# Two transformer layers in one launch: flat reads for the sums of squares, a hinted branch on SyncE, and four pieces of work in other places

## The chip, the cores and the metric

The kernel runs on one core of a Trainium2 chip. Its engines are TensorE (PE in the profile; its weight loads are listed apart, as PEld), VectorE (DVE), ScalarE (ACT), GpSimd (POOL) and SyncE (SP), which here only issues DMAs. Each engine runs its own instructions in their order and waits for the others by semaphores. The metric is the device time of one launch in microseconds, the median of the runs.

## The reference

Two layers, each an attention block and a gated block, with the same weights in both layers. There are 2048 tokens, 448 features, 16 heads of 28 features, 1792 hidden features, all in float32.

```python
x = A_x                                             # 1 x 2048 x 448
for layer in range(2):
    qkv = layernorm(x) @ wqkv                       # 448 x 1344, 16 heads
    p = softmax(q @ k.T * 28 ** -0.5)               # 2048 x 2048 for each head
    x = x + (p @ v) @ wo
    y = layernorm(x)
    x = x + (sigmoid(y @ w_gate) * (y @ w_up)) @ w_down
```

## The kernel before

**Number formats.** Most products are made of float16 halves: an operand is a high part and the rest that the high part leaves, and three products of such parts add up to one. A weight matrix is scaled by a power of two that comes from the sum of its squares; the exact sum does not matter, only its binary exponent.

**Stages of a layer.** `project` makes the heads' queries, keys and values, for four blocks of 512 tokens. `attend` runs over the 16 heads and in each over 16 chunks of 128 keys. `out_project` applies `wo`. `gated` runs over the four blocks and, in each, over seven pairs of hidden tiles. The order of the instructions on every engine is the order in which the program writes them; nothing is rescheduled, except that `attend` works out from a rule how far the second products may run.

**Products by seven.** In `gated`, and for most of the queries and keys of layer 1, a product of 2 x 2 quarters is made with seven products and sums of quarters. A block's operands for that are made by its *half steps*, in `half_steps`: `r11`, `t1`, `t2`, `t3` and so on, each a subtraction or two on DVE (lines 443, 459 and 462) and a conversion on ACT (lines 451 and 453). The first of them, `r11`, is the first that reads the block's transposed values `xraw`, and so it waits for the DMA that gathers them. The half steps of a next block are laid between the products of a current one: `portions` says how many of them stand at each of six points (0 to 5) of each pair. Within a pair of `gated`, point 2 lies just ahead of the additions on DVE (line 1956) that read the banks `side`, and point 5 at the pair's end, behind the sums of hidden operands (lines 1831 to 1838).

**From layer 0 to layer 1.** The end of `gated` also prepares the next layer. `go_on` is called between the last second products and issues on SP: the store of the third block's transposed values (`xt_scr`, line 389), their gather (`xraw`, lines 397 and 399), and the load of the value weights (`wv`, line 740). SP's DMAs are issued in order; one that waits holds back those behind it. In `project` of layer 1, `vals(0, ...)` makes the values of the first block (line 1071) and `vals(1, ...)` those of the second (lines 641 to 643), into PSUM banks 3, 0, 1 and 6. Bank 6 held the squared norms `qnorm` of the second block's queries; `fin` takes their maxima on DVE (line 859).

**The branch.** A flag that DVE computes decides whether exact row maxima are needed. It is read by every engine (line 1211), which then branches (line 1212, not into the long body in these runs). Behind the branch SP issues the load of a head's guard rows (line 773), which the first scores of the first head need. `expect_jump` puts a branch hint into the program for PE: for layer 0's branch at the program's start, for layer 1's behind layer 0's branch.

**Attention.** Score units (128 keys by 512 queries, line 1507, banks `sc`) are taken three at a time; ACT makes their exponentials (line 1522), PE multiplies these with the values (line 1558). A few units of each head go *aside*: DVE makes their exponentials with a polynomial (lines 1532 to 1541). `ASIDE` says at which chunk of a head an aside unit is scored, and which chunk and query block it is; the bank `aside` is the one in which the head before kept its result, so it is free once DVE has read that (line 1587). The same DVE queue also prepares the weights of `gated` and of layer 1 during layer 0's attention: first sums of squares (class `Measure`, line 1268, before attention, and class `Prepare`, line 1398, in heads 0 and 1), then splits into sums of quarters (lines 255 to 264).

**Reads for the sums of squares.** A part of a matrix is read as rows on partitions, with `load_rows`: three DMAs for 448 rows, the last 64 rows twice (lines 216 and 219).

Of the kernel before, what the change touches and what calls it, by code (L numbers as in the profile page):

```python
# [12 lines left out]
BF16 = mybir.dt.bfloat16  # L13
F16 = mybir.dt.float16
I32 = mybir.dt.int32
AF = mybir.ActivationFunctionType
# [3 lines left out]
P = 128  # L20
S = 2048
D = 448
# [7 lines left out]
NF = F // P  # L30
# [36 lines left out]
ASIDE = {1: ((6, 15, 1),), 2: ((4, 10, 3), (9, 15, 1)), 3: ((4, 9, 3), (8, 13, 1), (12, 15, 2))}  # L67
FEW = "2222222222222223"


TAIL = (0, 1, 3, 2, 5, 4, 6)

PAIRS_QK = ((0, 1), (4, 5), (2, 6))
ALONE = 3
SUMS_AT = ((("w", 3), 74), (("u", 0), 122), (("u", 6), 236))

# [46 lines left out]
def interleaved_layers(ctx: ExitStack, tc: tile.TileContext, x_in, wqkv, wo, w_gate, w_up,  # L123
                       w_down, out):
    nc = tc.nc
# [87 lines left out]
    def load_rows(dst, src, c0, n, queue=nc.sync, second=None):  # L213

        for a, b in ((0, 2), (2, 3)) if second else ((0, 3),):
            (second if a else queue).dma_start(
                dst[:, a:b, :], src[a * P:b * P, c0:c0 + n].rearrange("(s p) n -> p s n", p=P))
        for r in (0, 64):
            (second or queue).dma_start(dst[r:r + 64, 3, :], src[384:448, c0:c0 + n])

    def split(hi, lo, raw):
# [559 lines left out]

    def expect_jump(layer):

        tc.mark_branch_hint_location(f"loose{layer}", hint="LikelyTaken",
                                     engines=[mybir.EngineType.PE])

# [6 lines left out]
    def project(layer, wq, begun):  # L793
# [355 lines left out]
        else:  # L1149
# [85 lines left out]
    class Measure:  # L1235
# [9 lines left out]
        def read(self, n=1):  # L1245
            for _ in range(n):
                kind, j = self.to_read.popleft()
                t = big.get("raw", [P, 2048])
                n = {"o": 4, "d": min(4, NF - 4 * j), "gu": 0}[kind]
                v = t[:, 0:n * D].rearrange("p (s n) -> p s n", n=D)  # L1250
                queue = nc.sync if kind == "o" or j < 3 and kind == "d" else nc.gpsimd
                if kind == "gu":
# [8 lines left out]
                self.rows.append((kind, t, n * D))  # L1261

        def add(self):
            kind, t, n = self.rows.popleft()
            m, n = {"o": (3, n), "d": (6, n), "gu": (4, 1024)}[kind]
            v = t[:, 0:n]
            junk = big.get("junk", [P, 2048], BF16)
            nc.vector.tensor_tensor_reduce(junk[:, 0:n], v, v, 1.0, sums[:, m:m + 1],
                                           op0=ALU.mult, op1=ALU.add,
                                           accum_out=self.part[:, 0:1])  # L1270
            big.put_next(junk)
            nc.vector.tensor_copy(sums[:, m:m + 1], self.part[:, 0:1])
            if kind == "gu":
                junk = qrt.get("junk", [P, 1024], BF16)
                nc.scalar.activation(junk, t[:, 1024:2048], AF.Square, accum_out=sums[:, 5:6])
                qrt.put(junk)
            big.put(t)
# [26 lines left out]
    class Prepare:  # L1304
# [41 lines left out]
        def read(self, kind, j):  # L1346
# [25 lines left out]
        def view(self, t, kind):  # L1372
            if kind == "gu":
                return t.rearrange("p (w s c) -> p w s c", w=2, s=4)
            if kind in "guq":
# [103 lines left out]
    def attend(layer, values, heads, last_values, gate, wq):  # L1479
# [294 lines left out]
    def gated(layer, first, wt, wq):  # L1774
# [311 lines left out]
        if not last:  # L2086
# [48 lines left out]
    def portions(b, p):  # L2135
# [100 lines left out]
```

## Time and profile before

| what | value |
|---|---|
| median of 3 runs | 1892.09 us (1891.86 to 1894.91) |
| the profiled execution's own time | 1893.09 us |
| its span, first to last instruction | 1891.4 us |
| granted TensorE clock | 1.000 |
| PE busy, PEld busy | 1879.7 us (99%), 1378.1 us (73%) |
| DVE busy, ACT busy, POOL busy | 1482.7 us (78%), 1418.5 us (75%), 250.9 us (13%) |
| DMA | 278.70 MB, mean 147 GB/s |

Times inside the run are microseconds from the span's start. Layer 0's projection runs to about 118, its attention to about 568, its gated part to about 956; layer 1's projection runs to about 1054. In a row of the timeline stand the start, the duration, the engine, the line and operation, the tiles, how many equal instructions are merged, and in brackets the idle time before with what ended it. Matmuls overlap their successors, so a row's start is surer than its end.

### The profile page before, as it was taken

Reading aid. Unit: us, or ns where it says so; the run is one execution under the profiler, and the core shown is the slowest. Engines: PE = TensorE matmul, PEld = TensorE weight load, DVE = VectorE, ACT = ScalarE, POOL = GpSimd, SP = SyncE. Lnnn points to the kernel's source line nnn. Section 1 sums busy time; section 2 is a strip of 40 time slices with the busy share of each in tenths; the row PEclk is TensorE's granted clock in tenths of the full one; section 3 lists DMA queues with packets and bytes.
Section 4 is the critical chain, followed back from the end, with each engine's and each line's share of the span. In section 5 each row is a group of like instructions: output and inputs, shape, how many; then the busy total and the mean of one; then the engine's idle time right before and its main releaser. Section 6 shows DMA issues by size and latency. Waiting matters only on the chain. (4 is left out here: it accounts for less than half of the span.)

```text
span 1891.4 us, 57180 instructions
## 1 busy us (share of the span) xinstructions
PE 1879.7 (99%) x24531; PEld 1378.1 (73%) x24531; DVE 1482.7 (78%) x2996; ACT 1418.5 (75%) x1873; POOL 250.9 (13%) x487
## 2 busy tenths in 40 slices
PE   9999999999999999999999999999999999999999
PEld 4456655556556899998977566765568768999999
DVE  7758999998997887787767587787778688877664
ACT  6569999999993655555557899999999747555541
POOL 3023122222202111111110000000000021111110
PEclk9999999999999999999999999999999999999999
DMA  7676454344333755646573421122110256566553
GB/s 251 190 217 160 133 159 124 121 134 127 115 108 87 267 199 213 221 185 245 192 222 117 102 52 45 34 52 52 29 49 17 74 164 227 200 228 223 209 208 142
DMA packets 117335, 278.70 MB, mean 147 GB/s; under 512 B 14574, under 2 KB 72686, under 8 KB 116944
## 3 DMA queue, kind: packets, MB, share of 16 engines
q0 software_dynamic: 33616, 165.92, 24.5%
q1 hardware_dynamic: 82304, 107.66, 20.1%
q8 instruction: 194, 3.18, 0.7%
q10 hardware_dynamic: 1152, 1.38, 0.3%
q14 instruction: 69, 0.57, 0.1%
HBM read 213.43 MB, written 53.08 MB: 141 GB/s over the span
## 5 line engine op out<-in xcount | busy, mean ns | idle before, releaser
L1522 ACT ACTIVATE prob_s<-sc 128x1536 f32<-128x1536 f32 (+1 forms) x657 | 888.8, 1479 | 8.7 <-PE sc L1507 6.7
L1558 PE MATMUL acc<-prob_s,val_s 128*32 128x256 f32 (+3 forms) x7700 | 579.5, 384 | 0.8 <-issue 0.8
L1507 PE MATMUL sc<-qp_s 114*32 114x512 f16 x7868 | 562.4, 379 | 0.2 <-DMA qp_s<-qk_scr 0.2
L631 PEld LDWEIGHTS <-gu_s 128*128 128x128 f16 x4368 | 426.8, 98 | 48.4 <-issue 2.5
L1507 PEld LDWEIGHTS <-qp_s 114*32 114x32 f16 x8192 | 290.2, 95 | 191.0 <-issue 80.8
L1558 PEld LDWEIGHTS acc<-prob_s,val_s 128*32 128x32 f32 x7700 | 291.9, 110 | 126.9 <-issue 12.1
L631 PE MATMUL chain<-xwide_s,gu_s 128*128 128x256 f16 x2016 | 247.5, 273 | 0.0
L1867 PE MATMUL dnp<-dn_s,hparts_s 128*128 128x224 f16 x2184 | 245.9, 259 | 0.0
L1867 PEld LDWEIGHTS <-hparts_s 128*128 128x128 f16 x2184 | 210.2, 98 | 5.1
L1538 DVE SCALAR_TENSOR_TENSOR power_q<-power_q,expo_q 128x512 f32<-128x512 f32 x243 | 168.2, 692 | 8.3
L1940 ACT COPY one_q<-chain 128x256 f32<-128x256 f32 x224 | 82.1, 372 | 112.4 <-PE chain L631 111.9
L1956 DVE TENSOR_TENSOR one_q<-side,one_q 128x512 f32<-128x512 f32 x112 | 72.1, 685 | 94.7 <-PE side L631 94.5
L631 PE MATMUL side<-xshort_s,gu_s 128*128 128x256 f16 x1120 | 140.6, 273 | 2.4 <-DVE one_q L1956 2.4
L1748 POOL DMA_DIRECT2D gu_s<-gu_parts x104 | 55.9, 538 | 441.6 <-PE side L631 427.6
L1820 ACT CAST hparts_s<-hsums_q 128x256 f16<-128x256 f32 (+1 forms) x152 | 71.5, 485 | 37.2 <-DVE hsums_q L1832 23.6
L1558 PE MATMUL acc<-power_q,val_s 128*32 128x256 f32 (+3 forms) x300 | 94.2, 396 | 0.0
L631 PE MATMUL side<-xwide_s,gu_s 128*128 128x256 f16 x672 | 91.7, 273 | 0.0
L1587 DVE STREAM_TRANSPOSE oturned_q<-acc 128x512 f32<-128x512 f32 x32 | 22.9, 717 | 82.4 <-PE acc L1558 82.1
L616 PE MATMUL qkp<-xhl_s,wqk_s 128*128 128x512 f16 x385 | 86.6, 379 | 0.9 <-ACT wqk_s L236 0.6
L1967 ACT ACTIVATE one_q<-one_q 128x512 f32<-128x512 f32 x56 | 35.3, 630 | 63.8 <-DVE one_q L1956 63.6
L1532 DVE TENSOR_SCALAR expo_q<-aside,base 128x512 f32<-128x512 f32 x81 | 60.5, 747 | 22.2 <-PE aside L1507 21.7
L1824 DVE TENSOR_TENSOR hparts_s<-hsums_q,hparts_s 128x256 f16<-128x256 f32 (+1 forms) x152 | 72.6, 516 | 6.0 <-ACT hparts_s L1820 6.0
(259 smaller groups left out, 2393.9 us busy)
## 6 DMA issues: line engine op xcount, KB each, us to landing
gu_s<-gu_parts POOLq DMA_DIRECT2D x104, 800.0 KB, 6.0
dn_s<-dn_parts POOLq DMA_DIRECT2D x42, 784.0 KB, 7.5
qp_s<-qk_scr SPq DMA_DIRECT2D x96, 224.0 KB
gu_parts<-pack_s POOLq DMA_DIRECT2D x14, 800.0 KB, 3.8
xt_scr<-xs_s SPq DMA_DIRECT2D x48, 224.0 KB
xraw_s<-xt_scr SPq DMA_DIRECT2D x12, 768.0 KB
qk_scr<-qkhl_q SPq DMA_DIRECT2D x35, 256.0 KB
qp_s<-qk_scr SPq DMA_DIRECT2D x64, 112.0 KB
```

Of the source, the lines that this page charges most:

```text
L616: nc.tensor.matmul(pm, w, x, start=(i == 0), stop=(i == len(terms) - 1))
L631: nc.tensor.matmul(pm, a, x, start=(first and i == 0), stop=(i == len(terms) - 1), skip_group_check=True)
L1507: nc.tensor.matmul(ps[32 * j:32 * j + 32, :], hd.k[:, keys], hd.q[:, qb * W:(qb + 1) * W], start=True, stop=True, tile_position=(0, 32 * j))
L1522: nc.scalar.activation(prob[:, 0:n, :], ps[:, 0:n, :], AF.Exp, scale=exp_scale)
L1532: nc.vector.tensor_scalar(y, ps, base2[:, 0:1], -126.0, op0=ALU.mult, op1=ALU.max)
L1538: nc.vector.scalar_tensor_tensor(p, p, c[k], y, op0=ALU.add, op1=ALU.mult)
L1558: nc.tensor.matmul(acc[qb * VC:(qb + 1) * VC, s], v[:, kc % TB, h, :], probs[c * NB + qb][:, s], start=(kc == 0 and a == 0), stop=(kc == N ...
L1820: nc.scalar.copy(to[:, :, 0], a)
L1824: nc.vector.tensor_tensor(to[:, :, 1], a, to[:, :, 0], op=ALU.subtract)
L1867: nc.tensor.matmul(pm, a[:, x, t], w[:, p, y], start=(begin and n == 0 and (j == 0 or alone)), stop=(n == 2), skip_group_check=True)
L1940: nc.scalar.copy(to, pm)
L1956: nc.vector.tensor_tensor(one[m], side[m], one[m], op=ALU.add)
```

## The change

- **Flat reads.** For the sums of squares a weight matrix is read as one flat run of memory cut into 128 equal pieces, one for each partition: one DMA of 128 x 896 numbers (`CHUNK`) where three stood, 128 x 1568 for `wo`, three of 128 x 1792 and one of 128 x 896 for `w_down`. No row is read twice. The reductions on DVE become 896 wide where they were 1024, and 1568 where `wo`'s was 1792.
- **SP's hint.** Behind layer 0's branch SP too gets a hint for layer 1's branch.
- **A half step.** In pair 3 of the last block of layer 0's `gated`, the half step at point 2 goes to point 5. It is `r11` of the next layer's first block.
- **Value weights.** `load_values` is called ahead of `third.gather`, no longer behind it.
- **Norm maxima.** In `vals(1, ...)` of layer 1, `fin` stands ahead of the half step `h3[2]` (`t2` of the last block), no longer behind it.
- **Asides of head 8.** In layer 0's head 8 the two aside units are scored at chunks 5 and 10; they were at 4 and 9. Which units they are does not change.

```diff
+BEHIND_SUMS = 8, ((5, 10, 3), (10, 15, 1))
+CHUNK = D * NF // 7
...
+    def flat(w):
+        return w.rearrange("r c -> (r c)").rearrange("(p n) -> p n", p=P)
...
-    def expect_jump(layer):
+    def expect_jump(layer, also=[]):
...
-                                     engines=[mybir.EngineType.PE])
+                                     engines=[mybir.EngineType.PE] + also)
...
-            vals(1, b1, {0: both(*h3[0:2]), 1: both(h3[2], fin), 2: both(*h3[3:5]),
+            vals(1, b1, {0: both(*h3[0:2]), 1: both(fin, h3[2]), 2: both(*h3[3:5]),
...
-                expect_jump(1)
+                expect_jump(1, [mybir.EngineType.SP])
...
                 if kind == "gu":
-                    v = t.rearrange("p (w s c) -> p w s c", w=2, s=4)
                     for i, w in enumerate((w_gate, w_up)):
-                        load_rows(v[:, i], w, 0, 2 * P, queue)
+                        queue.dma_start(t[:, i * n:(i + 1) * n], flat(w)[:, 0:n])
                 elif kind == "o":
-                    load_rows(v, wo, 0, D, queue)
+                    n = D * D // P
+                    queue.dma_start(t[:, 0:n], flat(wo))
                 else:
-                    queue.dma_start(v, w_down[j * 512:j * 512 + n * P, :].rearrange(
-                        "(s p) n -> p s n", p=P))
+                    n = min(2 * n, NF * D - 2 * n * j)
+                    queue.dma_start(t[:, 0:n], flat(w_down)[:, 2 * CHUNK * j:2 * CHUNK * j + n])
...
                 for i, w in enumerate((w_gate, w_up)):
-                    load_rows(self.view(self.next, kind)[:, i], w, j * 2 * P, 2 * P, nc.gpsimd)
+                    nc.gpsimd.dma_start(self.next[:, i * CHUNK:(i + 1) * CHUNK],
+                                        flat(w)[:, j * CHUNK:(j + 1) * CHUNK])
...
-            self.add(4, raw[:, 0:1024])
-            self.add(5, raw[:, 1024:2048])
+            for i in range(2):
+                self.add(4 + i, raw[:, i * CHUNK:(i + 1) * CHUNK])
...
-            for at, kc, qb in ASIDE[n]:
+            for at, kc, qb in (BEHIND_SUMS[1] if few and h == BEHIND_SUMS[0] else ASIDE[n]):
...
-                             [third.gather, wq.load_values], [], [], []])
+                             [wq.load_values, third.gather], [], [], []])
...
-                     3: {0: 1, 1: 1, 2: 1, 5: 1}, 4: {1: 1, 2: 1, 5: 2}, 5: {1: 1, 2: 2, 5: 3},
+                     3: {0: 1, 1: 1, 5: 2}, 4: {1: 1, 2: 1, 5: 2}, 5: {1: 1, 2: 2, 5: 3},
```

The order on DVE in pair 3 of layer 0's last block, before (`t_q` from `xraw_s` alone is `r11`; the additions that free the banks `side` are line 1956; the line numbers of the changed program are a few higher):

```order
L328 BN_AGGR mv_17770<-st_3_17816 128x2
L443 TENSOR_TENSOR t_q_17852<-xraw_s_17657 128x256 x2
L1956 TENSOR_TENSOR one_q_17748<-side_17746,one_q_17748 128x512
L1956 TENSOR_TENSOR one_q_17749<-side_17747,one_q_17749 128x512
L1970 SCALAR_TENSOR_TENSOR one_q_17748<-one_q_17749,one_q_17748 128x512
```

and in the changed program, at the pair's end (`t_q` from `xraw_s` alone is `r11` again, `xwide_s` and the last `t_q` are `t1`):

```order
L1840 TENSOR_TENSOR hsums_q_17869<-one_q_17723,two_q_17725 128x256
L1841 TENSOR_TENSOR hsums_q_17869<-two_q_17725,hsums_q_17868 128x256
L448 TENSOR_TENSOR t_q_17893<-xraw_s_17632 128x256 x2
L464 TENSOR_TENSOR xwide_s_17890<-xraw_s_17632,xwide_s_17890 128x256 x2
L448 TENSOR_TENSOR t_q_17900<-xraw_s_17632,t_q_17893 128x256 x2
```

The two subtractions of `r11` went from ahead of the additions, which now follow the `BN_AGGR` directly, to behind the last sum of the pair; its two conversions on ACT moved with them, to just ahead of `t1`'s.

SP's queue at the layer's end, before:

```order
L389 DMA xt_scr_18663<-xs_s_18538 32x14x128 x4
L397 DMA xraw_s_18684<-xt_scr_18663 128x3x512
L399 DMA xraw_s_18684<-xt_scr_18663 64x512
L740 DMA wv_s_18687<-v_parts 128x3584
L906 DMA qk_scr<-qkhl_q_18975 256x1x256 x2
```

and now:

```order
L394 DMA xt_scr_18638<-xs_s_18513 32x14x128 x4
L745 DMA wv_s_18659<-v_parts 128x3584
L402 DMA xraw_s_18661<-xt_scr_18638 128x3x512
L404 DMA xraw_s_18661<-xt_scr_18638 64x512
L911 DMA qk_scr<-qkhl_q_18950 256x1x256 x2
```

The load of `wv` stands between the stores and the gather. It takes the buffer that the gather had, and no longer stands behind the gather's wait for the stores.

DVE's queue in `vals(1, ...)` of layer 1, before (`t_q` and `xwide_s` are the last block's half steps):

```order
L443 TENSOR_TENSOR t_q_19451<-xraw_s_19254,t_q_19444 128x256 x2
L462 TENSOR_TENSOR xwide_s_19441<-t_q_19444,xwide_s_19441 128x512
L443 TENSOR_TENSOR t_q_19469<-xraw_s_19254 128x256 x2
L859 TENSOR_REDUCE peaks_18869<-qnorm_19258 16x1
L859 TENSOR_REDUCE peaks_18869<-knorm_19259 16x1
```

and now:

```order
L448 TENSOR_TENSOR t_q_19426<-xraw_s_19229,t_q_19419 128x256 x2
L864 TENSOR_REDUCE peaks_18844<-qnorm_19233 16x1
L864 TENSOR_REDUCE peaks_18844<-knorm_19234 16x1
L467 TENSOR_TENSOR xwide_s_19416<-t_q_19419,xwide_s_19416 128x512
L448 TENSOR_TENSOR t_q_19449<-xraw_s_19229 128x256 x2
```

The two maxima moved ahead of three instructions of `t2`.

More of the change, by code (lines that the diff above doesn't have):

```diff
@@ L1248, in read @@
                 t = big.get("raw", [P, 2048])
-                n = {"o": 4, "d": min(4, NF - 4 * j), "gu": 0}[kind]
-                v = t[:, 0:n * D].rearrange("p (s n) -> p s n", n=D)
                 queue = nc.sync if kind == "o" or j < 3 and kind == "d" else nc.gpsimd
+                n = CHUNK
                 if kind == "gu":
-                    v = t.rearrange("p (w s c) -> p w s c", w=2, s=4)
                     for i, w in enumerate((w_gate, w_up)):
-                        load_rows(v[:, i], w, 0, 2 * P, queue)
+                        queue.dma_start(t[:, i * n:(i + 1) * n], flat(w)[:, 0:n])
                 elif kind == "o":
-                    load_rows(v, wo, 0, D, queue)
-                else:
-                    queue.dma_start(v, w_down[j * 512:j * 512 + n * P, :].rearrange(
-                        "(s p) n -> p s n", p=P))
-                self.rows.append((kind, t, n * D))
+                    n = D * D // P
+                    queue.dma_start(t[:, 0:n], flat(wo))
+                else:
+                    n = min(2 * n, NF * D - 2 * n * j)
+                    queue.dma_start(t[:, 0:n], flat(w_down)[:, 2 * CHUNK * j:2 * CHUNK * j + n])
+                self.rows.append((kind, t, n))
         def add(self):
             kind, t, n = self.rows.popleft()
-            m, n = {"o": (3, n), "d": (6, n), "gu": (4, 1024)}[kind]
+            m = {"o": 3, "d": 6, "gu": 4}[kind]
             v = t[:, 0:n]
@@ L1273, in add @@
             if kind == "gu":
-                junk = qrt.get("junk", [P, 1024], BF16)
-                nc.scalar.activation(junk, t[:, 1024:2048], AF.Square, accum_out=sums[:, 5:6])
+                junk = qrt.get("junk", [P, n], BF16)
+                nc.scalar.activation(junk, t[:, n:2 * n], AF.Square, accum_out=sums[:, 5:6])
                 qrt.put(junk)
@@ L1372, in view @@
         def view(self, t, kind):
-            if kind == "gu":
-                return t.rearrange("p (w s c) -> p w s c", w=2, s=4)
             if kind in "guq":
```

## The prediction

> **What bounds the kernel now.** I read the page first, then TensorE's waits, then the timeline of PE and of its releaser around each wait that the change touches.
>
> ```profile
> span 1891.4 us, 57180 instructions
> PE 1879.7 (99%) x24531; PEld 1378.1 (73%) x24531; DVE 1482.7 (78%) x2996; ACT 1418.5 (75%) x1873; POOL 250.9 (13%) x487
> ```
>
> ```profile
> PE side L631 <- DVE one_q L1956: 2.4, 1, 2.4
> ...
> PE acc L1558 <- issue: 0.8, 1, 0.8
> PE vp L1071 <- DMA wv_s<-v_parts: 0.6, 1, 0.6
> ...
> PE vp L641 <- DVE peaks L859: 0.5, 1, 0.5
> PE sc L1507 <- DMA qp_s<-qk_scr: 0.2, 1, 0.2
> PE aside L1507 <- DVE oturned_q L1587: 0.2, 1, 0.2
> ```
>
> TensorE is busy nearly from end to end, so the time is its work plus its waits, and a shorter wait shortens the run unless a later one takes the time back. The change removes no matmul. Five of these six waits stand just where it moves something; the sixth ("issue") has no releaser. So the sum is made wait by wait. Its base is the profiled execution, 1893.09 us (span 1891.4); the median of the runs, 1892.09, lies 1.00 below.
>
> **The half step (`r11` of layer 1's first block).** PE first, then DVE:
>
> ```profile
> 883.64 0.74 PE L1867 MATMUL dnp<-dn_s,hparts_s 128*128 128x224 f16 x6
> 884.22 1.25 PE L631 MATMUL chain<-xshort_s,gu_s 128*128 128x256 f16 x10
> 885.31 0.74 PE L1867 MATMUL dnp<-dn_s,hparts_s 128*128 128x224 f16 x6
> 888.43 0.71 PE L631 MATMUL side<-xshort_s,gu_s 128*128 128x256 f16 x5 [2.38 <-DVE one_q L1956]
> ...
> 887.01 0.76 DVE L443 TENSOR_TENSOR t_q<-xraw_s 128x256 f32<-128x256 f32 x2 [4.85 <-DMA xraw_s<-xt_scr]
> 887.69 1.28 DVE L1956 TENSOR_TENSOR one_q<-side,one_q 128x512 f32<-128x512 f32 x2
> ...
> 892.70 0.42 DVE L1838 TENSOR_TENSOR hsums_q<-two_q,hsums_q 128x256 f32<-128x256 f32 x1
> ```
>
> DVE stands at `r11` for 4.85 us until the gather has landed; the additions that free the banks `side` are queued behind it, and PE waits for those. Six `dnp` matmuls let the next group start 0.58 later (883.64 to 884.22), so `side` was due at 885.89 and came at 888.43: 2.54 lost, the bracket's 2.38 plus 0.16 by which a matmul's shown end lies behind the next start. At point 5 DVE meets `r11` behind L1838, which ends at 893.12, or 890.58 once the 2.54 are gone: 3.6 behind the landing. Its 0.76 of work then lies in DVE's idle time (4.85 less 2.54 leaves 2.31). I take 2.54. Low end 1.6: the visible 2.38 less 0.76, should the later half steps delay PE by `r11`'s own time. Late next, if all goes: the value weights.
>
> **The value weights.** SP's queue, then DMA by stretch (share and GB/s last), PE, and the first reader of the gathered rows:
>
> ```profile
> 957.24 0.30 SPq L389 DMA_DIRECT2D xt_scr<-xs_s  x1
> 961.02 0.38 SPq L397 DMA_DIRECT2D xraw_s<-xt_scr  x1
> ...
> 962.30 0.59 SPq L740 DMA_DIRECT2D wv_s<-v_parts  x1
> ...
> 940.00:952.00 12.00, 12.00 (x127) 12.00 (x126) 3.22 (x6) 0.00 (x0) 1.92 (x6) 1.00 0.91 324
> 961.00:965.00 4.00, 4.00 (x39) 3.58 (x38) 3.83 (x8) 1.99 (x5) 1.52 (x4) 1.00 0.97 357
> ...
> 972.56 0.73 PE L1071 MATMUL vp<-wv_s,xwide_s 128*128 128x448 f16 x3 [0.60 <-DMA wv_s<-v_parts]
> 978.83 0.70 ACT L451 CAST xwide_s<-xraw_s 128x256 f16<-128x256 f32 x2
> ```
>
> `wv` is issued at 962.30, behind a gather that waits for its stores until 961.02, and PE waits 0.60 (0.76 with the 0.16) for it. In front of the gather it can go out right behind the last store (957.24 + 0.30), some 4.7 us earlier, with the gather's 448 x 512 float32 (0.92 MB) no longer ahead of it; PE's need moves up by 2.54 only. I take 0.76; low end 0, since the DMA engines are full here (shares 0.91 and 0.97). What pays is the gather: it now queues behind `wv`'s 128 x 3584 float16 (0.92 MB), 2.6 us at the 357 GB/s of that stretch. Its reader, ACT at 978.83, starts 6 us after `wv`, until now the last of these transfers, has let PE go at 972.56; the same bytes in another order are there by then too. Covered, cost 0; without that cover ACT's evacuation of `vp`, queued behind the conversion, would be late for PE, and SP's next stores with it.
>
> **The norm maxima.** DVE and PE:
>
> ```profile
> 1003.65 0.68 DVE L462 TENSOR_TENSOR xwide_s<-t_q,xwide_s 128x512 f16<-128x512 f32 x1
> ...
> 1004.92 0.27 DVE L859 TENSOR_REDUCE peaks<-qnorm 16x1 f32<-16x128 f32 x1
> ...
> 1005.24 0.35 PE L641 MATMUL vp<-wv_s,xhl_s 128*128 128x448 f16 x1 [0.48 <-DVE peaks L859]
> ```
>
> PE loses 0.48 + 0.16 = 0.64 and was due at 1004.60. Ahead of `t2`, which starts at 1003.65, the maximum ends at 1003.92 instead of 1005.19. If the gain at `wv` brings PE 0.76 nearer but not DVE, PE is due at 1003.84, and some 0.1 is left. I take 0.55, ends 0.30 and 0.64. The half step behind it is delayed by twice 0.27; its readers are the products of the last block, two product rounds on.
>
> **SP's hint.** SP's wait at the branch, the branches themselves (duration min/median/max in ns, first and last start), SP's next DMA, PE:
>
> ```profile
> SPq L1212 <- SPq L1212: 2.9, 1, 2.9
> ...
> L1212 PEldq COMPARE_BRANCH  x2: 367/378/388, 112.5 to 1048.5; - x2
> L1212 SPq COMPARE_BRANCH  x2: 50/52/53, 112.5 to 1048.8; - x2
> ...
> L2232 PEldq BRANCH_PREFETCH_HINT  x2: 36/43/50, 0.9 to 112.9; - x2
> ...
> 1052.41 0.30 SPq L773 DMA_DIRECT2D qp_s<-g_scr  x1
> ...
> 1054.31 1.05 PE L1507 MATMUL sc<-qp_s 114*32 114x512 f16 x16 [0.25 <-DMA qp_s<-qk_scr]
> ```
>
> In layer 1 SP branches at 1048.8 and stands for 2.9 us with nothing to wait for but its own program; then it issues the guard rows, for which PE waits 0.25 (0.41 with the 0.16). PE, which was hinted for layer 0's branch, goes from the branch (112.5, 0.37 to 0.39 long) to its next instruction at 112.9, in about 0.1 us. If SP does likewise, the guard rows go out up to 2.9 earlier. I take 0.30, ends 0 and 0.41; one more instruction on SP in layer 0 costs 0.05, where PE waits for nothing.
>
> [...]
>
> **Asides of head 8.** PE and DVE:
>
> ```profile
> 348.69 0.40 PE L1507 MATMUL sc<-qp_s 114*32 114x512 f16 x4
> 349.26 0.40 PE L1507 MATMUL aside<-qp_s 114*32 114x512 f16 x4 [0.17 <-DVE oturned_q L1587]
> 349.48 0.62 PE L1558 MATMUL acc<-prob_s,val_s 128*32 128x256 f32 x8
> ...
> 348.49 0.72 DVE L1587 STREAM_TRANSPOSE oturned_q<-acc 128x512 f32<-128x512 f32 x1
> 358.02 0.75 DVE L1532 TENSOR_SCALAR expo_q<-aside,base 128x512 f32<-128x512 f32 x1
> ...
> L1522 ACT ACTIVATE prob_s<-sc 128x1536 f32<-128x1536 f32 x108 | 145.4, 1515 | 0.1
> ```
>
> The aside needs the bank that DVE reads until 349.21. A group of four takes 0.22 (349.26 to 349.48), so it was due at 348.91 and lost 0.35. One chunk later, four units or 1.3 groups of three, the bank is free. The second aside needs the first one read, until 358.77; one chunk later it doesn't wait either, but I can show no wait for it. The last row is ACT from 200 to 345: 108 exponentials in 145.4 us, 1.35 each, with 0.1 idle. So part of PE's delay lay in slack that ACT's pace leaves. I take 0.30, ends 0 and 0.6. DVE's order doesn't change, and it comes to the aside only at 358.02, so a later score costs nothing.
>
> **The flat reads.**
>
> ```profile
> L1398 DVE CUSTOM_DVE_ANT_0 junk_s<-raw_s,sums 128x1024 bf16<-128x1024 f32 x12 | 15.4, 1282 | 0.5
> 96.68 1.14 DVE L1268 CUSTOM_DVE_ANT_0 junk_s<-raw_s,sums 128x896 bf16<-128x896 f32 x1
> ...
> ...
> 169.90 0.59 PE L1558 MATMUL acc<-prob_s,val_s 128*32 128x128 f32 x7 [0.79 <-issue]
> ```
>
> DVE saves 12 times 1.282 - 1.14, 1.7 us; on POOL each of 14 parts takes one issue, not three. PE waits for neither in that stretch: before 349 its only wait in attention is the "issue" at 169.90. Worth 0. But the flat loads change the DMA traffic beside that "issue" wait, and it can go or come again elsewhere: ends -0.79 and +0.79.
>
> **The sum.** 2.54 + 0.76 + 0.55 + 0.30 + 0.30 = 4.45. 1893.09 - 4.45 = 1888.64, or 1887.6 on the scale of the median. All low ends together: 1.6 + 0.3 - 0.79 = 1.1, 1891.0; all high ends: 2.54 + 0.76 + 0.64 + 0.41 + 0.6 + 0.79 = 5.74, 1886.35.
>
> **Rivals.**
> - *The half step's gain is taken back by full DMAs.* From 940 to 965 their share is 0.91 to 0.97; if the weights of layer 1 land no earlier, PE waits for them and the 2.54 are lost: 1892.09 - 1.91 = 1890.2. For it: that share. Against: those loads are issued on releases by PE and DVE, which come 2.54 earlier as well.
> - *The hint does nothing on SP:* 1887.9.
> - *The "issue" wait goes with the denser reads:* 1892.09 - 4.45 - 0.79 = 1886.8.
> - *Slower: DVE becomes the bound of layer 0's last pairs.* `r11` runs later, and `t1` to the last half step crowd behind it; every addition that frees `side` would then be late again, once in each pair. It decides when more than the 2.31 of idle time is used up. To end at 0.2% slower it must cost 4.45 + 3.8 = 8.2 us, some 2 us in each of the last four pairs: 1895.9. Against it: `r11` is 0.76.
>
> **How the numbers follow.** The bound of what a measurement of this kernel tells from no change is 0.2%, 3.8 us: below 1888.3 is faster. Chances: forecast 0.58 (0.49 of it below 1888.3, which is only 0.7 away), hint idle 0.15 (0.10 of it below), "issue" gone 0.07, gain taken back 0.16, slower 0.04. Faster: 0.49 + 0.10 + 0.07 = 0.66; slower 0.04; same 0.30. The range runs from the high ends, with 0.4 for the spread of the runs, to just short of the taken-back case: 1885.9 to 1890.0.
>
> **What would show it.** In the changed profile PE's waits should have lost the row of 2.4 on `one_q`, that on `wv` and that on `peaks`; DVE should meet `r11` without waiting; `wv` should be issued some 4.7 us ahead of the gather's old place; SP's own wait at L1212 should fall from 2.9 to under 0.5 and the first scores follow the values at once. Wrong would be a new wait of PE between 890 and 1050, above all for `wsums`, `xhl` or bank `side`, or "issue" rows in heads 0 to 2.

## The result and the profile after

The changed kernel takes 1887.83 us (median of 17 runs, 1887.07 to 1889.86) against 1891.92 (17 runs, 1890.48 to 1894.94): the ratio is 0.9979, with a 95% interval from 0.9971 to 0.9986. That is 4.1 us shorter by the medians, and 0.2 us above the forecast of 1887.6. It lies inside the range. The experiments show that this agreement is partly luck: the terms for the half step and the value weights were too large, and the flat reads, set at nothing, made up for it.

The head of the page of the changed kernel, and TensorE's waits in it (engine, line, what ended the wait: total, count, longest):

```profile
span 1886.5 us, 57150 instructions
PE 1878.0 (100%) x24539; PEld 1391.4 (74%) x24539; DVE 1480.6 (78%) x2996; ACT 1417.3 (75%) x1873; POOL 232.9 (12%) x459
```

```profile
PE turn L565 <- DVE xn_s L365: 1.6, 1, 1.6
PE still L305 <- DVE warm L187: 1.2, 1, 1.2
PE qkp L621 <- ACT wqk_s L241: 0.6, 1, 0.6
PE acc L1561 <- issue: 0.3, 1, 0.3
PE aside L1510 <- DVE oturned_q L1590: 0.3, 1, 0.3
```

The waits for `one_q`, `wv`, `peaks` and `qp_s` are gone. "issue" is down from 0.8 to 0.3. The wait at the aside has gone from head 8, and one of 0.27 us stands at head 11 in its place. At the half step, DVE and TensorE in the timeline:

```profile
887.39 0.42 DVE L1841 TENSOR_TENSOR hsums_q<-two_q,hsums_q 128x256 f32<-128x256 f32 x1
887.73 0.75 DVE L448 TENSOR_TENSOR t_q<-xraw_s 128x256 f32<-128x256 f32 x2
...
884.67 1.25 PE L636 MATMUL side<-xshort_s,gu_s 128*128 128x256 f16 x10
```

DVE goes from the pair's last sum straight to `r11` without a wait, and the matmul on `side` that stood for 2.38 us follows the `dnp` matmuls at once. The value weights and the maxima, on SP, DVE and TensorE:

```profile
953.12 0.69 SPq L745 DMA_DIRECT2D wv_s<-v_parts  x1
956.46 0.38 SPq L402 DMA_DIRECT2D xraw_s<-xt_scr  x1
...
999.58 0.27 DVE L864 TENSOR_REDUCE peaks<-qnorm 16x1 f32<-16x128 f32 x1
...
1000.03 0.35 PE L646 MATMUL vp<-wv_s,xhl_s 128*128 128x448 f16 x1
...
1003.42 0.82 PE L636 MATMUL side<-xwide_s,wsums_s 128*128 128x256 f16 x6
1004.29 1.47 PE L636 MATMUL chain<-xwide_s,wsums_s 128*128 128x256 f16 x12
```

`vp` no longer waits for the maxima. But six matmuls on `side` let the next group start 0.65 later elsewhere (1008.63 to 1009.29 in the profile before); here it takes 0.87 (1003.42 to 1004.29). These 0.22 us are new. ACT converts the half step's `t_q`, which DVE now makes behind the maxima, and waits longer for it; first before, then now:

```profile
1005.03 0.62 ACT L453 CAST xwide_s<-t_q 128x512 f16<-128x512 f32 x1 [0.21 <-DVE t_q L443]
```

```profile
1001.35 0.62 ACT L458 CAST xwide_s<-t_q 128x512 f16<-128x512 f32 x1 [0.59 <-DVE t_q L448]
```

The copy that frees the bank `chain` stands behind it in ACT's queue, and TensorE, which now arrives earlier, meets it.

I lined the two traces up, matmul by matmul. TensorE gained 2.55 us at the half step, 0.81 at `wv`, 0.64 less 0.22 at the maxima, and 0.33 at the guard rows. The prediction had 2.54, 0.76, 0.55 and 0.30, so they agree within 0.13. That comparison misleads, though: it sets one execution beside one other.

### The profile page after: what moved, and what is told of

Its sections match the earlier page's. It is cut to its first block, busy times and chain, and to the rows that moved or that the text cites. A ratio compares the mean times of both kernels' runs of the same rounds, so it can differ in the third digit from the quotient of the medians.

```text
span 1886.5 us, 57150 instructions
## 1 busy us (share of the span) xinstructions
PE 1878.0 (100%) x24539; PEld 1391.4 (74%) x24539; DVE 1480.6 (78%) x2996; ACT 1417.3 (75%) x1873; POOL 232.9 (12%) x459
## 5 line engine op out<-in xcount | busy, mean ns | idle before, releaser
L1510 PEld LDWEIGHTS <-qp_s 114*32 114x32 f16 x8192 | 294.5, 96 | 184.2 <-issue 79.2
L1561 PEld LDWEIGHTS acc<-prob_s,val_s 128*32 128x32 f32 x7708 | 298.6, 110 | 117.4 <-issue 9.1
```

The costliest lines, as they stand in the source:

```text
L1510: nc.tensor.matmul(ps[32 * j:32 * j + 32, :], hd.k[:, keys], hd.q[:, qb * W:(qb + 1) * W], start=True, stop=True, tile_position=(0, 32 * j))
L1561: nc.tensor.matmul(acc[qb * VC:(qb + 1) * VC, s], v[:, kc % TB, h, :], probs[c * NB + qb][:, s], start=(kc == 0 and a == 0), stop=(kc == N ...
```

## The experiments

All comparisons of time are with runs of the kernel before on the same chip, whose medians were 1891.26, 1891.19 and 1891.35 us in the three groups of four. A few tenths of a microsecond can't be read from the times (the intervals are some 3 us wide). They can be read from the traces, so each of these kernels also serves as a further reading of every place that it leaves as it was.

### The half step alone, and all but the half step

```diff
-                     3: {0: 1, 1: 1, 2: 1, 5: 1}, 4: {1: 1, 2: 1, 5: 2}, 5: {1: 1, 2: 2, 5: 3},
+                     3: {0: 1, 1: 1, 5: 2}, 4: {1: 1, 2: 1, 5: 2}, 5: {1: 1, 2: 2, 5: 3},
```

This line alone was put into the kernel before (`half_step_alone`); and it alone was taken out of the changed kernel (`all_but_half_step`).

> Only the half step moves from point 2 to point 5; the rest is the kernel before. Theory (each wait counts by itself): TensorE's wait of 2.4 us for DVE's one_q is gone, its wait for wv stays between 0.5 and 0.9 us, those for peaks and for qp_s stay, and the run is 2.5 us shorter (2.2 to 2.8), about 1889.4 us against 1891.9. Rival (the gain is taken back by full DMAs): the rows of wv land no earlier than before, TensorE waits for them some 3 us instead of 0.6, and the run is less than 0.8 us shorter. Rival (DVE is the limit there): new waits for one_q in the pairs behind, and the gain is 1.7 us or less.

> The changed kernel with the half step put back at point 2. Theory: TensorE's wait of 2.4 us for one_q is back, the waits for wv, peaks and qp_s stay away, and the run is 2.5 us longer than the changed kernel, about 1890.3 us, 1.6 us shorter than before. Rival (the parts cover one another, so that what one gains the other can't): the run is less than 0.8 us shorter than before.

Alone: 1890.52 us, ratio 0.9994 (0.9985 to 1.0004). All but it: 1888.83 us, ratio 0.9986 (0.9977 to 0.9996). By the medians it brings 0.7 us alone, not 2.5, and the rest brings 2.4 without it, not 1.6; but the intervals (0.8 longer to 2.8 shorter, and 0.8 to 4.4 shorter) hold the expected values too, so the times alone don't decide. The wait on `one_q` is indeed gone in the first, and `wv` isn't waited for at all there, which speaks against full DMAs that take the gain back. In the second TensorE's wait has another size than before:

```profile
PE side L636 <- DVE one_q L1959: 1.1, 1, 1.1
```

What differs is how long the gather takes. DVE's `r11`, in `all_but_half_step`, then in `flat_alone` and in `asides_alone` (below), where it stands in its old place too:

```profile
884.11 0.76 DVE L448 TENSOR_TENSOR t_q<-xraw_s 128x256 f32<-128x256 f32 x2 [3.53 <-DMA xraw_s<-xt_scr]
```

```profile
885.32 0.76 DVE L447 TENSOR_TENSOR t_q<-xraw_s 128x256 f32<-128x256 f32 x2 [5.08 <-DMA xraw_s<-xt_scr]
```

```profile
885.75 0.76 DVE L444 TENSOR_TENSOR t_q<-xraw_s 128x256 f32<-128x256 f32 x2 [2.89 <-DMA xraw_s<-xt_scr]
```

SP had issued the gather at 873.54, 873.26 and 877.37: it took 10.6, 12.1 and 8.4 us until DVE could start, the same bytes each time. In all eight profiles that have `r11` in its old place, the core's DMA engines moved 3.2 to 3.4 MB between these two moments, the gather's 0.92 MB among them. The gather is in after about the same traffic each time; what differs is how fast that goes, from 377 GB/s in `asides_alone` down to 318 in `all_but_half_step` and 279 in `flat_alone`. Why the rate differs is open. These three ran on one chip, so the chip alone doesn't make it.

### The kernel before, once more

No edit: the kernel before, profiled a second time.

> The kernel before, unchanged, profiled once more. Theory (the waits for transfers are drawn anew in each execution): the waits for one_q (2.4 us in the first profile), wv (0.6), peaks (0.5) and qp_s (0.2) come out otherwise, by 0.3 us or more for at least two of them, while the wait at the aside of head 8 stays between 0.15 and 0.3 us and issue between 118 and 175 us at 0.5 to 1.5 us in all. Rival (one profile gives each wait): all six within 0.15 us of the first profile.

TensorE's waits in it, which are to be read against the first quotation of the prediction:

```profile
PE acc L1558 <- issue: 1.5, 2, 1.1
...
PE vp L641 <- DVE peaks L859: 1.2, 1, 1.2
PE side L631 <- DVE one_q L1956: 0.9, 1, 0.9
...
PE sc L1507 <- DMA qp_s<-qk_scr: 0.4, 1, 0.4
PE aside L1507 <- DVE oturned_q L1587: 0.3, 1, 0.3
```

The same program waits 0.9 us for `one_q` where it waited 2.4, 1.2 for `peaks` where it waited 0.5, and not at all for `wv`. One profile does not give the size of such a wait. So I collected each wait over all kernels that leave its cause in its old place (us, from TensorE's waits; a dash: moved there):

| kernel | `one_q` | `wv` | `peaks` | `qp_s` or issue at the first scores | issue, 118 to 175 |
|---|---|---|---|---|---|
| before | 2.4 | 0.6 | 0.5 | 0.2 | 0.8 |
| `before_again` | 0.9 | 0 | 1.2 | 0.4 | 1.5 |
| `half_step_alone` | - | 0 | 0.3 | 0.5 | 1.0 |
| `all_but_half_step` | 1.1 | - | - | - | - |
| `flat_alone` | 2.6 | 0 | 0.1 | 0 | - |
| `asides_alone` | 0.4 | 0 | 1.0 | 0.3 | 0.8 |
| `values_alone` | 1.4 | - | 1.1 | 0.3 | 1.4 |
| `maxima_alone` | 0.7 | 0 | - | 0.2 | 0.8 |
| `hint_alone` | 1.0 | 0.8 | 0.6 | - | 0.8 |
| `no_flat` | - | - | - | - | 0.5 |
| mean | 1.3 | 0.2 | 0.7 | 0.3 | 0.95 |

Where one of the four causes was moved, its wait (`one_q`, `wv`, `peaks`, `qp_s`) is 0 in every profile.

The same in stretches. From the end of layer 0's last head to layer 1's first scores, where those four parts lie, the four kernels that move none of them take 486.75 (before), 485.39 (`before_again`), 484.62 (`asides_alone`) and 485.68 us (`flat_alone`), 485.61 in the mean. The five that move all of them take 482.64 (the changed kernel), 482.50, 482.86, 482.50 and 482.89, 482.68 in the mean (`no_flat`, and three kernels below). The four parts together are worth 2.93 us, to about half a microsecond, since the four stretches without them lie up to 2.1 us apart. The pair of profiles before and after shows 4.11, because before's own stretch was 1.14 us longer than the mean. The rows that bound this stretch, of the changed kernel (DVE's turning of a head's result, TensorE's first scores):

```profile
566.35 0.72 DVE L1590 STREAM_TRANSPOSE oturned_q<-acc 128x512 f32<-128x512 f32 x1 [1.64 <-PE acc L1561]
...
1048.99 0.83 PE L1510 MATMUL sc<-qp_s 114*32 114x512 f16 x12
```

and of the kernel before the first of them (its first scores, at 1054.31, are in the prediction):

```profile
567.56 0.72 DVE L1587 STREAM_TRANSPOSE oturned_q<-acc 128x512 f32<-128x512 f32 x1 [1.71 <-PE acc L1558]
```

### Value weights, maxima and hint, each alone

```diff
-                             [third.gather, wq.load_values], [], [], []])
+                             [wq.load_values, third.gather], [], [], []])
```

> Only the value weights move ahead of the gather. Theory of the prediction: the wait for wv of 0.6 us, and that alone, is gone, and TensorE passes that place 0.76 us nearer than in the profile before. Rival (the wait of 0.6 us belonged to the one execution that was profiled: four runs with the value weights in the old and the new place all passed it without a wait): nothing is gained, and the place is passed as in the kernels whose value weights stayed. Both expect the run within 1 us of before; TensorE's wait for one_q may lie anywhere from 0.4 to 2.6 us, as the runs so far have it.

1890.83 us, ratio 1.0001 (0.9991 to 1.0010). TensorE passes the place without a wait, but so do five of the seven profiles with the value weights in the old place. The rival fits better than the theory: the wait is there in two executions of seven (0.6 and 0.8), some 0.2 us in the mean.

```diff
-            vals(1, b1, {0: both(*h3[0:2]), 1: both(h3[2], fin), 2: both(*h3[3:5]),
+            vals(1, b1, {0: both(*h3[0:2]), 1: both(fin, h3[2]), 2: both(*h3[3:5]),
```

> Only the norm maxima move ahead of the half step. Theory: TensorE's wait for peaks, which was 0.5, 0.3, 0.1 and 1.0 us in the kernels that leave it in its place, is gone altogether, and no new wait above 0.25 us stands between there and the scores of layer 1. Rival: DVE is late by as much behind it, and the products of the sums behind wait 0.2 us or more. The run within 1 us of before either way.

1892.33 us, ratio 1.0007 (0.9998 to 1.0017); the time shows no gain. In the trace the wait for `peaks` is gone and nothing new stands behind it up to the first scores, where 0.2 us are left. The rival's delay comes in some of the kernels in which TensorE arrives earlier still: 0.22 us in the changed kernel, and in `no_asides` (below), which has every part but the asides, the profile names it:

```profile
PE chain L635 <- ACT one_q L939: 0.2, 1, 0.2
```

```diff
-                expect_jump(1)
+                expect_jump(1, [mybir.EngineType.SP])
```

> Only SyncE's hint. Theory: SyncE's own wait at the branch of layer 1 falls from 2.9 us to under 0.5, and TensorE doesn't wait for the guard rows (0.25 and 0.45 us in kernels without the hint). Rival (the hint does nothing): SyncE stands there for 2 to 3 us as before. The run 0 to 0.5 us shorter by the theory, the same by the rival.

1891.51 us, ratio 1.0001 (0.9991 to 1.0011). SP's own waits at the branch (total, count, longest) in this kernel:

```profile
SPq L1212 <- SPq L1212: 2.2, 2, 1.3
```

and in the changed one:

```profile
SPq L1217 <- SPq L1217: 1.1, 2, 0.7
```

Both waits of each row lie behind layer 1's branch, so their sum counts. Without the hint SP has one such wait, of 2.6 to 2.9 us in all seven profiles; with it, two or three that add up to 0.8 to 2.2 us in the seven. From the branch to the issue of the guard rows SP takes 3.3 to 3.6 us without the hint and 1.5 to 2.8 with it, 2.8 in `hint_alone`. The hint works on SP, less fully than I expected (under 0.5), and enough: no profile with it has TensorE wait for the guard rows, and six of the seven without it have a wait there, of 0.2 to 0.5 us. What SP stands for in those 2.6 to 2.9 us no run shows.

### The flat reads, alone, without, and in pieces

`flat_alone` is the kernel before with the edits of the flat reads (all lines of the change's diff with `CHUNK` or `flat`; the core of them below); `no_flat` is the changed kernel without them.

```diff
-                    load_rows(self.view(self.next, kind)[:, i], w, j * 2 * P, 2 * P, nc.gpsimd)
+                    nc.gpsimd.dma_start(self.next[:, i * CHUNK:(i + 1) * CHUNK],
+                                        flat(w)[:, j * CHUNK:(j + 1) * CHUNK])
```

> Only the flat reads of the whole weights for the sums of squares. Theory (the DMA traffic beside the instruction fetches decides): TensorE's wait put down to issue near 170 us falls from 0.79 to about 0.3 us as in the changed kernel, and the run is 0.3 to 0.6 us shorter. Rival (the wait differs from run to run by itself): the run is within 0.3 us of before, and the wait takes any value. Rival (DVE's shorter readings count, because DVE is busy without a break from 330 to 442 us): DVE's chain over that stretch is some 0.3 us shorter and the run with it.

> The changed kernel with the strided reads of the kernel before put back. Theory now (the flat reads are worth 1 to 2 us, since they take the load off the DMA engines while TensorE's instructions are fetched, and work off DVE where it sets the pace): TensorE's waits put down to issue between 118 and 175 us are back, 0.5 to 1.0 us together, and the run is 1.5 us longer than the changed kernel, about 1889.5 against 1888. Rival (the prediction's zero): no such wait above 0.3 us, and the run within 0.4 us of the changed kernel.

`flat_alone`: 1890.06 us, ratio 0.9993 (0.9984 to 1.0002). `no_flat`: 1889.58, ratio 0.9996 (0.9987 to 1.0006), so without the flat reads some 2.5 us of the changed kernel's gain of 4.1 are lost by the medians (0.9979 against 0.9996). The prediction's zero for this part is wrong. Where it lies is clear in the traces, in stretches of layer 0's attention and at the end (us; means of the kernels in each row; `asides_8_and_11`, described below, is left out of the middle column, since it moves something else there):

| | first scores to the end of head 1 | head 1 to head 11 | layer 1's last head to the end |
|---|---|---|---|
| strided reads (8 profiles) | 62.38 (61.74 to 62.96) | 278.93 (278.83 to 279.00) | 390.05 (389.97 to 390.24) |
| flat reads (4; the first and last column 5) | 60.96 (60.76 to 61.49) | 278.30 (278.22 to 278.37) | 390.64 (390.45 to 390.70) |
| flat reads in pieces (1) | 60.94 | 278.82 | 390.09 |

Shorter by 1.42 and by 0.63, longer by 0.59 at the end; with 0.1 between heads 11 and 15, some 1.5 us net. (Layer 1's heads are 0.24 shorter too, 447.06 to 446.82, but the two groups overlap there.)

*The first stretch.* TensorE's waits "for issue" there, 0.5 to 1.5 us in all eight profiles with strided reads, are 0 in every kernel with flat reads but the changed one, which keeps 0.3. To separate the transfers from DVE's work, the flat reads were cut up again:

```diff
                 for i, w in enumerate((w_gate, w_up)):
-                    nc.gpsimd.dma_start(self.next[:, i * CHUNK:(i + 1) * CHUNK],
-                                        flat(w)[:, j * CHUNK:(j + 1) * CHUNK])
+                    for c in range(0, CHUNK, 256):
+                        e = min(CHUNK, c + 256)
+                        nc.gpsimd.dma_start(self.next[:, i * CHUNK + c:i * CHUNK + e],
+                                            flat(w)[:, j * CHUNK + c:j * CHUNK + e])
```

> The changed kernel, with each flat read of a part of w_gate and w_up cut into four transfers of at most 256 columns (1 KB a row and transfer, as the strided reads had), so that DVE still reads 896 columns but the transfers are as small and POOL issues as many as before the change. Theory A (the size of the transfers makes the gain between 118 and 175 us): TensorE's waits put down to issue there come back, 0.5 us or more, and that stretch is some 1.2 us longer than in the changed kernel; the gain of 0.4 to 0.7 us from 175 to 450 us, where DVE sets the pace, stays; the run about 1 us longer than the changed kernel. Theory B (DVE's shorter reading makes it all): no such wait above 0.35 us, and both stretches as in the changed kernel.

1888.93 us, ratio 0.9986 (0.9977 to 0.9995). No wait for issue, and 60.94 us as with whole reads: theory A falls, it is not the size of the transfers and not POOL's issues. The same 20 us in `no_flat`, in the changed kernel and in `flat_in_pieces` (busy time of PE, PEld, DVE, ACT, POOL; then clock, DMA share, GB/s):

```profile
150.00:170.00 20.00, 19.45 (x350) 10.99 (x342) 18.15 (x34) 20.00 (x16) 8.94 (x16) 1.00 0.75 197
```

```profile
150.00:170.00 20.00, 19.68 (x352) 14.22 (x346) 18.21 (x35) 20.00 (x16) 2.26 (x4) 1.00 0.59 176
```

```profile
150.00:170.00 20.00, 20.00 (x361) 11.59 (x357) 17.93 (x34) 20.00 (x16) 11.24 (x22) 1.00 0.65 177
```

In pieces POOL is busier than with strided reads. What the two flat kernels share is less traffic (176 and 177 GB/s against 197: no row is read twice), and DVE's shorter readings:

```profile
L1401 DVE CUSTOM_DVE_ANT_0 junk_s<-raw_s,sums 128x896 bf16<-128x896 f32 x12 | 13.8, 1149 | 0.3
```

which saves 12 times 0.133, 1.6 us. The traces speak against DVE's readings. Lined up with `flat_alone`, the kernel before loses 0.35 us near 133 us, where no row shows a wait, and 1.05 near 170, at the row of 0.79, and 0.15 in all the rest of this stretch; at neither place does TensorE wait for DVE. What it waits for near 170 no row names. I take it to be its own instructions, which no run shows by itself; the figures that I go by are these. The trace's DMA records have a kind `instruction`, with 194 packets of 16 KB and 68 or 69 of 8 KB. I take the larger ones to be TensorE's, which has 49062 of the program's 57180 instructions. In all nine profiles with the wait near 170 (0.3 to 1.1 us), TensorE goes on 2.5 to 2.8 us after such a packet begins. The packet's start can be measured against one matmul that stands shortly ahead of the place: it lies 0.6 to 1.2 us before that matmul with strided reads, 1.3 in the changed kernel, which keeps 0.3 us of wait, and 1.8 to 2.9 in the five profiles without the wait. So the packet comes late beside the strided reads. That the lighter traffic lets it come earlier fits these figures, but no run changes the traffic alone.

*Head 1 to head 11.* Both theories said that the pieces keep this gain too. They don't (278.82). From 330 to 442 us DVE has no gap above 0.06 us, so a DVE instruction that takes longer there should move TensorE. POOL and DVE in the kernel before, near 344 us:

```profile
343.97 0.75 POOL L1369 DMA_DIRECT2D raws_s<-in_B_w_gate_dram  x1
344.71 0.77 POOL L1367 DMA_DIRECT2D raws_s<-in_B_w_gate_dram  x1
...
344.13 1.01 DVE L261 TENSOR_SCALAR pack_s<-sums_q,up 128x512 f16<-128x512 f32 x2
345.06 0.67 DVE L261 TENSOR_SCALAR pack_s<-raws_s,up 128x512 f16<-128x512 f32 x1
```

and in the changed kernel:

```profile
343.20 0.74 POOL L1374 DMA_DIRECT2D raws_s<-in_B_w_gate_dram  x1
344.63 0.78 POOL L1372 DMA_DIRECT2D raws_s<-in_B_w_gate_dram  x1 [0.69 <-issue]
...
343.36 0.87 DVE L266 TENSOR_SCALAR pack_s<-sums_q,up 128x512 f16<-128x512 f32 x2
344.15 0.48 DVE L266 TENSOR_SCALAR pack_s<-raws_s,up 128x512 f16<-128x512 f32 x1
```

Where POOL issues DMAs all along, DVE's packing takes 0.33 us more (0.14 and 0.19). With the flat reads POOL stands for 0.69 us for no reason that the profile shows, just then, and DVE's two rows take 0.87 and 0.48. The pieces have the long pair again (1.01 and 0.67, POOL without a gap). Fifteen other packings of 128x512 from `raws_s` in the trace of before, with no POOL issue beside them, take 0.48 us. But one at 261.10, beside a POOL issue of 0.77 us for other reads (line 1362), takes 0.47, so an issue beside it does not lengthen every packing. What lengthens it near 344 us, and what makes POOL stand, no run shows. The pieces read the same flat runs without POOL's gap, so I don't take it for a gain of flat reads as such (that was not tested). The 0.33 are half of the 0.63. Of the rest, TensorE gains 0.16 us near 224 us and 0.10 near 314 over `no_flat`, where no row shows a wait; the cause is open.

*The end.* In four of the five kernels with whole flat reads DVE has a gap between the two additions that free `side`, which strided reads don't have there:

```profile
1597.17 0.69 DVE L1959 TENSOR_TENSOR one_q<-side,one_q 128x512 f32<-128x512 f32 x1 [0.20 <-issue]
```

TensorE loses 0.3 us at it (its lead over the kernel before falls from 5.59 to 5.29 us between 1590 and 1615). In pieces the gap lies at 642 us instead, and the 0.3 us are lost there. The gap does not explain all: `flat_alone` lacks it and loses 0.3 us at the same place too, and the same gap at 699 and 921 us, in all five kernels, costs TensorE nothing. The other 0.3 us lie behind the last matmul: from its start to the end of the span it is 4.08 us in those four kernels, against 3.67 to 3.77 in the other ten. Most of this is a stop of POOL among its last instructions, 0.33 us where the other ten have 0.04; its cause is open.

### The asides

```diff
-            for at, kc, qb in ASIDE[n]:
+            for at, kc, qb in (BEHIND_SUMS[1] if few and h == BEHIND_SUMS[0] else ASIDE[n]):
```

`asides_alone` has only this, `no_asides` everything else. `asides_8_and_11` is the changed kernel with head 11 at the later chunks too:

```diff
-BEHIND_SUMS = 8, ((5, 10, 3), (10, 15, 1))
+BEHIND_SUMS = (8, 11), ((5, 10, 3), (10, 15, 1))
...
-            for at, kc, qb in (BEHIND_SUMS[1] if few and h == BEHIND_SUMS[0] else ASIDE[n]):
+            for at, kc, qb in (BEHIND_SUMS[1] if few and h in BEHIND_SUMS[0] else ASIDE[n]):
```

> Only the two asides of head 8 one chunk later. Theory (a wait of TensorE counts by itself): the wait of 0.2 us at 349 us goes, none comes in its place, and the run is 0.3 us shorter. Rival (DVE, busy without a break from 330 to 442 us, sets the pace): the wait comes again at the aside of head 11, near 432 us, with 0.2 to 0.4 us, and from there on TensorE stands within 0.1 us of where it stood before.

> The changed kernel with the asides of head 8 back in their old place. Theory (the move shifts a wait from head 8 to head 11, and DVE sets the pace between them): no wait at head 11; at head 8 0 to 0.3 us; TensorE stands at 450 us within 0.3 us of the changed kernel, and the run within 0.5 us of it. Rival (the move gains 0.3 us by itself): 0.3 us longer, with a wait of 0.2 us or more at head 8.

> The changed kernel with the asides of head 11 one chunk later too. Theory: the wait of 0.27 us at head 11 goes, and since DVE has idle time again behind 441 us, none comes in its place: TensorE passes 450 us 0.3 to 0.4 us earlier, and the run is that much shorter than the changed kernel. Rival (DVE sets the pace there as well): the wait comes again in heads 12 to 14, and nothing is gained.

`asides_alone`: 1892.5 us, ratio 1.0003 (0.9994 to 1.0012). `no_asides`: 1887.69, ratio 0.9977 (0.9968 to 0.9986). `asides_8_and_11`: 1887.96, ratio 0.9981 (0.9972 to 0.9990). In every kernel with head 8 alone moved a wait of 0.3 us stands at head 11, as in the changed kernel:

```profile
431.78 0.40 PE L1510 MATMUL aside<-qp_s 114*32 114x512 f16 x4 [0.27 <-DVE oturned_q L1590]
```

From head 1 to head 11 the move saves 0.13 us with strided reads (278.97, the mean of six, to 278.83 and 278.84) and 0.11 with flat ones (278.35 to 278.24): the wait is shifted, not removed, because DVE sets the pace between. Lined up, `asides_alone` gains 0.60 us over the kernel before at head 8's two asides (340 to 361 us), loses 0.17 near 376 and 0.47 at head 11's aside near 432. With the flat reads no row shows a wait at head 8 in the old place (`no_asides`); lined up, the move gains 0.4 us there and loses 0.35 at head 11. With head 11 moved as well, both waits are gone and the stretch takes 277.92, 0.34 less than in the changed kernel; no wait came in heads 12 to 14. In the times neither variant can be told from the changed kernel (0.9977 and 0.9981 against 0.9979), so none of these versions is shown to beat it.

## Why the prediction was right, and where it wasn't

**The total** was 1887.6 forecast, 1887.83 measured. By the means over profiles the parts are worth 2.93 (half step, value weights, maxima, hint), 0.12 (asides) and some 1.5 (flat reads), some 4.55 in all, against 4.1 by the medians, which is inside the ratio's interval (2.7 to 5.5 us).

**The half step** was sized 2.54, ends 1.6 and 2.54. The mechanism holds: DVE stands for the gather, the additions queue behind it, and at point 5 nothing waits. But the wait is 0.4 to 2.6 us by profile, 1.3 in the mean, 1.5 with the 0.16 that the prediction adds. The term was mis-sized, and its low end was drawn from the wrong cause: it allowed for later half steps, not for a gather that takes 8 to 12 us.

**The value weights** were sized 0.76. Only two of seven profiles have the wait; some 0.25 in the mean. The low end, 0, was the better number. The gather behind the weights cost nothing, as argued.

**The norm maxima** were sized 0.55. Over seven profiles the wait is 0.7, 0.85 with the 0.16, and 0.1 to 0.3 come back at the bank `chain` in three of the seven profiles with the maxima moved, the changed kernel (0.22) among them. The prediction put the half step's delay at nothing since its readers come two rounds on; but ACT converts it at once, and what came late was ACT's copy that frees `chain`, queued behind.

**SP's hint** was sized 0.30; the mean wait that it removes is 0.3, 0.4 with the 0.16. The rival that it does nothing is ruled out by SP's own waits; by the time alone it can't be told (1.0001). SP's waits did not fall below 0.5 as forecast: they are 1.1 in the changed kernel.

**The asides** were sized 0.30 and bring 0.12. At head 8 itself the gain is 0.60, the prediction's high end. The step that failed is "DVE's order doesn't change, so a later score costs nothing": the prediction looked at ACT's pace and not at DVE's, which has no idle time from 330 to 442 us, so that TensorE meets it again at head 11.

**The flat reads** were set at 0 with ends of 0.79 either way, and bring some 1.5. The prediction named the mechanism of the larger part (the wait for issue beside this traffic, and the rival in which it goes, 1886.8) and gave it 7 chances in 100. It failed in taking one profile's single wait of 0.79 for the whole price: that very profile loses 1.4 us in the stretch against `flat_alone`, and the second profile of the same kernel shows 1.5 of wait.

**Why the sum held** is luck. The terms for the four parts add up to 4.15, read from an execution whose stretch was 1.14 us longer than the mean; they are worth 2.93. The flat reads made up for it. Nor does taking off 1.00 for the median at the end repair such terms, since nothing ties that microsecond to these waits: up to its first scores the same execution took 117.75 us, less than any of the other thirteen (118.06 to 120.14). With correct sizes for the four parts and the asides, and the prediction's zero for the flat reads, the forecast would have been 1892.09 - 2.93 - 0.12 = 1889.0, no change clear of the prediction's own bound of 1888.3.

**The other rivals.** Full DMAs did not take the half step's gain back: in the changed kernel TensorE is busy all through the same stretch (busy time of PE, PEld, DVE, ACT, POOL, clock, DMA share, GB/s) at a share of 1.00, and waits for no weights:

```profile
940.00:952.00 12.00, 12.00 (x128) 12.00 (x126) 3.10 (x5) 0.00 (x0) 1.57 (x6) 1.00 1.00 334
```

DVE did not become the bound of layer 0's last pairs: no wait for `one_q` in any kernel with `r11` at point 5.

## What to carry to other kernels

A wait behind a transfer can differ much between executions of one program (2.4 and 0.9 us here): profile the same kernel several times, or read the place in every variant that leaves it alone, before a term is made of it. What the profiled execution lies above the median says nothing of where it lost it; compare it with other profiles stretch by stretch. Where two engines keep pace with TensorE, ask which has no idle time around a small wait; moving the work on the other side only shifted the wait along here (0.60 us gained at head 8, 0.17 and 0.47 lost again behind it).

## What the runs showed of the hardware

- One gather of 0.92 MB, issued at the same place in programs that are alike there, took 8.4 to 12.1 us until its reader could start, in eight profiles; the core's DMA engines moved 3.2 to 3.4 MB meanwhile each time.
- The branch hint works on SyncE: its waits behind layer 1's branch were 2.6 to 2.9 us in all without it and 0.8 to 2.2 with it, in seven profiles each.
- Near 170 us, behind no branch, TensorE stood 0.3 to 1.1 us in nine profiles of fourteen for nothing that the profile names, and each time went on 2.5 to 2.8 us after a 16 KB packet of the kind `instruction` began. That it waited for its own instructions is my reading.
- One `TENSOR_SCALAR` on DVE, from float32 to float16 on 128x512, took 0.67 us near 345 us, where POOL issued DMAs all along, and 0.48 in the changed kernel, where POOL stood beside it. Fifteen others with no issue beside them took 0.48 in the trace of before, but one at 261 us took 0.47 beside an issue.
- Gaps that no wait explains stand at the same instruction in kernels with the same reads (0.20 us on DVE at 699 and 921 us, 0.69 on POOL at 344, in all five with whole flat reads), and elsewhere in the kernels with other reads. TensorE lost 0.3 us beside one of them (DVE, 1597 us, four of the five), and nothing beside the two at 699 and 921.
